# Spreading the fetched key pairs inside a chunk and cutting the value and output products into pieces

## Chip, core, metric

One NeuronCore of a Trainium2 chip runs the whole program. The metric is the device time of one execution in microseconds (us); several executions are timed and their median is given. The profile is one further execution, taken by the hardware profiler. TensorE (PE) multiplies matrices into PSUM banks; its weight loads are listed as PEld. VectorE (DVE), ScalarE (ACT) and GpSimd (POOL) work elementwise, and SyncE (SP) issues nearly all DMAs.

## The reference

Attention with squared ReLU instead of softmax feeds a gated unit with a causal convolution over five rows. B = 8, S = 3200, D = 256, and the query and key width is 64.

```python
scores = z @ z.T / S                      # queries and keys are the same z
attn = np.maximum(scores, 0) ** 2
x = u * (attn @ v)
gate = sigmoid(sum(conv_w[k] * x[t - 4 + k] for k in range(5)))
out = (gate * (x @ w_val)) @ w_out
```

All is float32. The kernel keeps that precision by splitting each operand of a product into a high part and a remainder and multiplying three combinations, called terms.

## The kernel before, in words

**Tiling.** The 3200 rows of a batch are 25 tiles of 128. Queries are taken in seven chunks of 4, 4, 4, 4, 3, 3, 3 tiles (the last batch: 4, 4, 4, 4, 4, 3, 2), so a product has 512, 384 or 256 columns. Keys are taken in 13 pairs of tiles (the last has one tile). A **step** is one chunk of queries with one pair of keys; 8 x 7 x 13 steps follow each other in one order written out by hand (`steps`, L762; the loop from L883), and `place` (L253) gives a pair's position in its chunk.

**Computed and fetched steps.** Scores are symmetric. A **computed** step multiplies queries and keys on TensorE (`scores`, L376), takes ReLU and square on ScalarE (L523, L524), splits into `ah` (ScalarE's cast, L526, or VectorE's, L528) and `al` (VectorE, L532), and, where a later chunk will need the mirrored block, turns it on VectorE (L431) and stores it in DRAM (L453). A **fetched** step (`mirrored`, L419) loads that block into `m` (L468) and only splits it, without scores. Steps `halves` and `split` do half of each. In the order before, pairs stand by number, so the fetched ones, which are the low ones, stand at the head of a chunk: 0, 2, 4, 6, 8, 9 and 11 of them in chunks 0 to 6 of the batches 1 to 6. Two exceptions are `new_first` (L248: chunk 3 of the last batch has them at the end) and the last chunk of all.

**One step on TensorE.** At step s TensorE multiplies the weights of step s with v into two accumulator banks `acc0`, `acc1` (12 products in slots of the chunk's width) and makes the scores of step s + 3 (`AHEAD`). Scores contract over 64 rows only, so two of them run side by side in the upper and the lower 64 rows of the array (`side_by_side`, L342, products at L350). So that the form need not change, the products with v are then done in 64-row form too, in two halves: `attend` part 0 lets the upper rows fill one bank and the lower rows the other, part 1 swaps them. Before part 1, `turn_round` (L361) makes TensorE wait until part 0 is done with the banks. If the pair at s + 3 is fetched, the step has no scores and runs with the full 128 rows (`attend_whole`, L566, the branch `if not halved`, L893).

**What else stands in the steps.** For the chunk before, `gated` (L591, `x`) multiplies the accumulators by u on VectorE at the end of its last step, which frees the banks for the next chunk; then come the convolution (L637), the value product (`value`, in two parts at step 5, or `value_whole`, L674) into the banks `misc`, and the gate (L642, L687 to L696). For the chunk before that, the output product stands at step 0 (`project`, two parts with one term of scores between them, or `project_whole`, L729), and ScalarE copies the result (`ob`, L748) at steps 1 and 2. `zq` is the chunk's queries in the order that a product reads contiguously (`z_order`, L225), written three steps before the chunk (five before chunk 0); where `has_copy` (L218) is false the scores read them strided from `zhl`. All other work hangs on steps through `at_step` (L777), in the order of the queues; `m` is fetched six steps before it is used, three before its split.

Of the kernel before, what the change touches and what calls it, by code (L numbers as in the profile page):

```python
# [17 lines left out]
def attn_glu_kernel(  # L18
# [30 lines left out]
    B, S, D = u.shape  # L49
# [195 lines left out]
    def own(b, c, x):  # L245
        return all_firsts[b][c] // 2 + x

    def new_first(b, c):  # L248


        return b == B - 1 and c == 3

    place = {}  # L253
    for b in range(B):
        for c in range(n_chunks):
            order = list(range(NP))
            if two_pairs(b, c):
                order.append(order.pop(own(b, c, 1)))
            if new_first(b, c):
                new = [i for i in order if sum(pairs[i]) > all_firsts[b][c]]  # L260
                new.sort(key=lambda i: pairs[i][0] < all_firsts[b][c])
                order = new + [i for i in order if i not in new]
# [141 lines left out]

    mirror, m_in, turned_, to_keep = {}, {}, {}, []

    def keeps(b, c, g):

        return c < g and (b > 0 or c > 1 or (c == 1 and g >= 5))
# [9 lines left out]
    def mirrored(b, c, i):  # L419
        return all(keeps(b, all_homes[b][t][0], c) for t in range(pairs[i][0], sum(pairs[i])))  # L420

    def turn(b, c, i, a):

# [130 lines left out]
                out_.append((acc, vp[:, j, hs], ap_[:, j], first and j == m == 0, last and j == n - 1 and m == 2))  # L554
        return out_

    def attend(b, c, i, part):

        p = place[b, c, i]
        x = (p + part) % 2  # L560
        sides = (attend_list(b, c, i, h, part == 0 and p == 0, part == 1 and p == NP - 1) for h in (x, 1 - x))
        turn_round("acc", sides, part)

    def attend_whole(b, c, i, h):
        for out_, st, mv, first, last in attend_list(b, c, i, h, place[b, c, i] == 0, place[b, c, i] == NP - 1):
# [88 lines left out]
                )  # L654
        return out_

    def value(b, c, part):
        if part == 0:
            pvs[b, c] = [ps.tile([P, 512], F32, name=f"misc{e}", bufs=1) for e in range(DH)]
        sides = (value_list(b, c, e, part == 0, part == 1) for e in (part, 1 - part))  # L660
        turn_round("misc", sides, part)

    def two_banks(spare, names="misc"):

# [49 lines left out]
    def project(b, c, part):  # L714
        if part == 0:
            pos[b, c] = [ps.tile([P, 512], F32, name=f"misc{x}", bufs=1) for x in range(DH)]
        sides = (project_list(b, c, x, part == 0, part == 1) for x in (part, 1 - part))
        turn_round("misc", sides, part)

    def project_whole(b, c, spare=False):  # L720
        pos[b, c] = two_banks(spare, "acc" if spare else "misc")
# [47 lines left out]
    def project_at(b, c):  # L769

        return 2 if (b, c) == (0, 2) else 0

    todo = {}
# [39 lines left out]
    for b in range(B):  # L813
        for c in range(n_chunks):
            s0 = start(b, c)
            nxt = s0 + NP
            for h in range(DH):
                for part in range(2):
                    at_step(max(s0 + U_LOAD[b > 0][c], 2) + 2 * h + part, u_load, b, c, h, part)
            if (b, c) != LAST:  # L820
                for r, fn, args in BEHIND:
                    late = b == c == 0 and fn in (gate_value, gate_value_high, gate_value_low)
                    at_step(nxt + (min(r + FIRST_VALUE - VALUE, FIRST_LAST[r]) if late else r), fn, b, c, *args)
                for x in range(DH):
                    at_step(nxt + project_at(*steps[nxt][:2]) + 1 + x, out_copy_before, b, c, x)
            at_step(max(s0 + U_PREP[b > 0][c], 6), u_prep, b, c)

            met = start(b, 0) + all_firsts[b][c] // 2 - AHEAD
            if has_copy(b, c):
                for x in range(2):  # L830
                    at_step(s0 - (5 if c == 0 or new_first(b, c) else 3), z_order, b, c, x)
            if b == 0:
                met -= c == 1
                at_step(met - 5, z_load, b, c)
                early = 1 if c == 0 else 0
                at_step(met - 3 - early, z_turn, b, c)
                at_step(met - 2 - early, z_high, b, c)
                at_step(met - 1 - early - (c >= 2), z_low, b, c)
            else:
                s1 = Z_FROM[b][c] + start(b - 1, 4)  # L840
                at_step(s1, z_load, b, c)
                late = 1 if b == 1 else 0
                at_step(s1 + late + 3, z_turn, b, c)
                at_step(s1 + late + 4, z_high, b, c)
                at_step(s1 + late + 5, z_low, b, c)
            for i in range(NP):
                if mirrored(b, c, i) or halves(b, c, i) or split(b, c, i):
                    at_step(s0 + place[b, c, i] - AHEAD - FETCH + (new_first(b, c) and halves(b, c, i)), m_fetch, b, c, i, first=True)
# [27 lines left out]
        for j in range(n + 1):  # L876
            at_step(first + j // step, next, fn, None)

    held = []
    with tc.manual_schedule():  # L880
        zeros = sb.tile([P, CW], F32R, name="zeros", tag="gvl", bufs=1)
        nc.vector.memset(f32(zeros), 0.0)
        for s in range(min(todo), END + 1):  # L883
            b, c, i = steps[s] if s >= 0 else (0, 0, 0)
            p = s % NP if s >= 0 else s
            ahead = steps[s + AHEAD] if 0 <= s + AHEAD < N else None
            halved = ahead and not mirrored(*ahead)
            terms = list(range(3))
# [3 lines left out]
            behind = steps[s - NP][:2] if s >= NP and p == (FIRST_VALUE if s < 2 * NP else VALUE) else None  # L892
            if not halved:  # L893
                if before:
                    project_whole(*before)
                for h in range(DH if 0 <= s < END else 0):
                    attend_whole(b, c, i, h)
                if behind:
                    for e in range(DH):
                        value_whole(*behind, e)  # L900
            else:
                if before:
                    project(*before, 0)
                    scores(*ahead, terms[:1])
                    project(*before, 1)
                    terms = terms[1:]
                if s >= NP and p == 0 and not before:

                    scores(*ahead, terms)
                    for h in range(DH):  # L910
                        attend_whole(b, c, i, h)
                    terms = ()
                elif s >= 0:
                    attend(b, c, i, 0)
                if behind:
                    value(*behind, 0)
                if terms:
                    scores(*ahead, terms)
                    if s >= 0:
                        attend(b, c, i, 1)  # L920
                if behind:
                    value(*behind, 1)
            if p == NP - 1:
                for h in range(DH):
                    gated(b, c, h)
                while held:
                    held.pop(0)()
# [85 lines left out]
```

## Time and profile before

| what | value |
|---|---|
| median of 3 timed runs | 2292.95 us (2292.73 to 2294.2) |
| the profiled execution, first to last instruction (span) | 2290.8 us |
| granted TensorE clock | 1.000 |
| DMA | 466.39 MB, mean 204 GB/s |

The profiled execution is known by its span alone. In the rows of the profile, an engine's busy time is given with its share of the span and its number of instructions; a group of instructions has its line, engine, operation, output and inputs, shape and count, then busy time and the mean duration of one in ns, and after the second bar the idle time just before them with what ended it. A row of waits reads: engine, tile and line that waited, what it waited for, us in total, times, longest. A row of the timeline reads: start and length in us, engine, line, operation, tiles, shape, count, and in brackets the idle time before. A row of a stretch gives its length and the busy time of PE, PEld, DVE, ACT and POOL with instruction counts, then the clock and the DMA's share and rate.

### The profile page before, as it was taken

Reading aid. Unit: us, or ns where it says so; the run is one execution under the profiler, and the core shown is the slowest. Engines: PE = TensorE matmul, PEld = TensorE weight load, DVE = VectorE, ACT = ScalarE, POOL = GpSimd, SP = SyncE. Lnnn points to the kernel's source line nnn. Section 1 sums busy time; section 2 is a strip of 40 time slices with the busy share of each in tenths; the row PEclk is TensorE's granted clock in tenths of the full one; section 3 lists DMA queues with packets and bytes.
Section 4 is the critical chain, followed back from the end, with each engine's and each line's share of the span. In section 5 each row is a group of like instructions: output and inputs, shape, how many; then the busy total and the mean of one; then the engine's idle time right before and its main releaser. Section 6 shows DMA issues by size and latency. Waiting matters only on the chain.

```text
span 2290.8 us, 47245 instructions
## 1 busy us (share of the span) xinstructions
PE 2283.8 (100%) x18625; PEld 2004.0 (87%) x18625; DVE 1818.1 (79%) x2393; ACT 1777.2 (78%) x2404; POOL 55.7 (2%) x108
## 2 busy tenths in 40 slices
PE   9999999999999999999999999999999999999999
PEld 7888988889888998889988899888998889988889
DVE  7877888788878878788787887888877887778776
ACT  8988778776888768887688776887768877687765
POOL 0000000000000000000000000000000000000000
PEclk9999999999999999999999999999999999999999
DMA  7265897778977889688887789868897788966753
GB/s 133 65 158 149 213 261 206 205 199 246 255 185 202 213 246 251 171 211 223 242 237 191 198 226 247 229 187 207 236 239 214 199 222 233 237 189 171 197 150 100
DMA packets 688592, 466.39 MB, mean 204 GB/s; under 512 B 355313, under 2 KB 639217, under 8 KB 688369
## 3 DMA queue, kind: packets, MB, share of 16 engines
q1 hardware_dynamic: 687168, 463.10, 76.4%
q8 instruction: 146, 2.39, 0.4%
q14 instruction: 78, 0.63, 0.1%
q10 hardware_dynamic: 1200, 0.26, 0.1%
HBM read 251.73 MB, written 211.48 MB: 202 GB/s over the span
## 4 chain that ended last, share of the span: by engine, by line
PE 96%; ACT 1%; DVE 1%; SPq 1%; DMA 1%; issue 0%; DVEq 0%; ACTq 0%
PE acc L350 45%; PE acc L566 29%; PE s L350 10%; PE misc L350 6%; PE misc L729 4%; PE misc L674 2%; SPq L166 0%; DMA u_raw<-in_u_dram 0%; ACT a L524 0%; SPq L292 0%; ACT a L523 0%; ACT ah L526 0%; DVE al L532 0%; DMA v_raw<-in_v_dram 0%; DMA z_raw<-in_z_dram 0%
## 5 line engine op out<-in xcount | busy, mean ns | idle before, releaser
L350 PE MATMUL acc<-ah,v_hl 64*128 64x512 f32 (+1 forms) x6624 | 1071.4, 375 | 0.7 <-DVE v_hl L308 0.7
L350 PEld LDWEIGHTS acc<-ah,v_hl 64*128 64x128 f32 x6624 | 620.1, 184 | 112.2 <-issue 11.7
L566 PE MATMUL acc<-ah,v_hl 128*128 128x384 f32 (+2 forms) x2288 | 639.6, 355 | 0.2 <-DVE x L596 0.2
L350 PE MATMUL acc<-al,v_hl 64*128 64x512 f32 (+1 forms) x3312 | 626.3, 374 | 0.0
L532 DVE TENSOR_TENSOR al<-a,ah 128x1024 fp32r<-128x1024 f32 (+3 forms) x387 | 422.9, 1093 | 223.1 <-ACT ah L526 215.3
L523 ACT ACTIVATE a<-s 128x1024 f32<-128x1024 f32 (+3 forms) x387 | 356.0, 920 | 146.1 <-PE s L350 144.5
L566 PEld LDWEIGHTS acc<-ah,v_hl 128*128 128x128 f32 x2288 | 417.5, 188 | 47.3 <-ACT a L486 5.7
L532 DVE TENSOR_TENSOR al<-m,ah 128x768 fp32r<-128x768 f32 (+2 forms) x303 | 307.9, 1024 | 121.3 <-ACT ah L526 120.6
L566 PE MATMUL acc<-al,v_hl 128*128 128x384 f32 (+2 forms) x1144 | 402.9, 352 | 0.0
L524 ACT ACTIVATE a<-a 128x1024 f32<-128x1024 f32 (+3 forms) x387 | 371.3, 959 | 12.3
L526 ACT CAST ah<-m 128x768 fp32r<-128x768 f32 (+2 forms) x303 | 266.7, 892 | 145.6 <-DMA m<-mir 108.7
L350 PEld LDWEIGHTS acc<-al,v_hl 64*128 64x128 f32 x3312 | 312.6, 184 | 46.9 <-DVE al L532 0.6
L526 ACT CAST ah<-a 128x1024 fp32r<-128x1024 f32 (+3 forms) x350 | 333.6, 953 | 11.1
L431 DVE STREAM_TRANSPOSE turned<-a 128x1024 f32<-128x1024 f32 (+3 forms) x318 | 320.1, 1011 | 25.6 <-DMA mir<-turned 24.7
L637 DVE SCALAR_TENSOR_TENSOR gate<-x,cw,gate 128x512 f32<-128x512 f32 (+2 forms) x448 | 303.5, 678 | 4.5 <-ACT gate L635 0.3
L350 PE MATMUL s<-zq,zhl 64*128 64x512 f32 (+3 forms) x2046 | 259.4, 356 | 0.0
L566 PEld LDWEIGHTS acc<-al,v_hl 128*128 128x128 f32 x1144 | 215.2, 188 | 15.1 <-DVE al L532 0.2
L350 PEld LDWEIGHTS s<-zq,zhl 64*128 64x128 f32 x2046 | 184.9, 184 | 29.4
L642 ACT ACTIVATE gate<-gate 128x512 f32<-128x512 f32 (+2 forms) x112 | 65.4, 584 | 47.5 <-DVE gate L637 47.3
L596 DVE TENSOR_TENSOR x<-acc,ut 128x512 f32<-128x512 f32 (+2 forms) x112 | 67.4, 629 | 38.4 <-PE acc L350 25.4
L316 ACT CAST v_made<-v_raw 128x512 fp32r<-128x512 f32 x97 | 55.9, 576 | 39.5 <-DMA v_kept<-v_made 38.4
L691 ACT CAST gvh<-gv 128x512 fp32r<-128x512 f32 (+2 forms) x112 | 64.0, 572 | 27.5 <-DVE gv L687 27.2
(120 smaller groups left out, 2020.1 us busy)
## 6 DMA issues: line engine op xcount, KB each, us to landing
m<-mir SPq DMA_DIRECT2D x191, 384.0 KB, 4.8
mir<-turned SPq DMA_DIRECT2D x340, 192.0 KB, 4.0
mir<-turned SPq DMA_DIRECT2D x188, 256.0 KB, 4.3
m<-mir SPq DMA_DIRECT2D x94, 512.0 KB, 6.1
v_hl<-v_kept SPq DMA_DIRECT2D x84, 512.0 KB, 6.6
v_kept<-v_made SPq DMA_DIRECT2D x71, 512.0 KB, 5.3
u_raw<-in_u_dram SPq DMA_DIRECT2D x264, 64.0 KB, 3.4
out_dram<-ob SPq DMA_DIRECT2D x33, 512.0 KB, 4.1
```

What stands on the lines that cost most here:

```text
L350: ins = nc.tensor.matmul(out_, st[r], mv[r], start=first, stop=last)
L431: nc.vector.transpose(into[:, t : t + m], a[:, j * w : (j + m) * w].rearrange("p (t m x) -> p t m x", t=m, x=BLK))
L523: nc.scalar.activation(a.rearrange("p (j x) -> p j x", j=2), s[:, :, :each], AF.Relu, scale=scale)
L524: nc.scalar.activation(a, a, AF.Square)
L526: nc.scalar.copy(hi, a)
L532: nc.vector.tensor_tensor(lo, a, f32(hi), op=ALU.subtract)
L566: nc.tensor.matmul(out_, st, mv, start=first, stop=last)
L596: nc.vector.tensor_tensor(x[:, h, HALO : HALO + w], accs[b, c][h][:, :w], ut[b, c][:, h, :w], op=ALU.mult)
L637: nc.vector.scalar_tensor_tensor(g, tap, cw[:, h, k : k + 1], g, op0=ALU.mult, op1=ALU.add)
L642: nc.scalar.activation(g, g, AF.Sigmoid)
L691: nc.scalar.copy(gvs[b, c][0][:, e, :w], gv_[b, c, e][:, :w])
L729: nc.tensor.matmul(out_, st, mv, start=first, stop=last)
```

## The change

In the chunks whose number of fetched pairs is a key of `MIRRORED_AT`, the fetched pairs take the listed places and the computed ones the rest, in their old order. `new_first` is gone. So most steps without scores (`lacks(s)`: the pair at s + 3 is fetched) now lie between the steps with scores.

A step without scores now runs in halves too when it is one of a chunk's `value_places` or `project_places`, or stands alone between two steps that do (`by_halves`). Between its two halves stands a piece of a product: the value product of the chunk before, cut into 2, 4 or 5 pieces over the steps 4 to 8 without scores, or part 1 of the output product, cut into as many pieces as there are such steps among 1 and 2, plus one at step 0 (part 0 and all terms of the scores then stand there without the one-term gap). A step without scores and without a piece does its first half and leaves its second (`left`) for the next step. Longer stretches without scores and pieces keep the 128-row form.

Around this, `zq` of these chunks is written five steps ahead, and the last two places of the chunk before read strided. The gate's steps move back by one or two where the last value piece is at step 7 or 8, the output copies go to step 2 where the output product ends there, and `attend` picks its side by a running switch.

```diff
     def has_copy(b, c, i=None):
-        if i is not None and new_first(b, c + 1) and place[b, c, i] == NP - 1:
+        if i is not None and place[b, c, i] >= NP - 2 and c < n_chunks - 1 and spread(b, c + 1):
             return False
...
+    MIRRORED_AT = {
+        2: (8, 9),
+        4: (7, 8, 9, 10),
+        6: (4, 7, 8, 9, 10, 11),
+        7: (4, 5, 7, 8, 9, 10, 11),
+        8: tuple(range(4, 12)),
+        9: tuple(range(4, 13)),
+    }
...
+    def spread(b, c):
+        n = sum(mirrored(b, c, i) for i in range(NP))
+        return n in MIRRORED_AT
...
+            if spread(b, c):
+                fetched = [i for i in order if mirrored(b, c, i)]
+                computed = [i for i in order if not mirrored(b, c, i)]
+                at_ = MIRRORED_AT[len(fetched)]
+                order = [(fetched if p in at_ else computed).pop(0) for p in range(NP)]
...
-    def attend(b, c, i, part):
+    way = [0]
+
+    def attend(b, c, i, part, again=False):
         p = place[b, c, i]
-        x = (p + part) % 2
+        if part and not again:
+            way[0] = 1 - way[0]
+        x = way[0]
...
-        turn_round("acc", sides, part)
+        turn_round("acc", sides, part and not again)
...
+    def cut(sides, piece, pieces):
+        out_ = []
+        for mms in sides:
+            lo, hi = (len(mms) * x // pieces for x in (piece, piece + 1))
+            out_.append(mms[lo:hi])
+        return out_
...
+    def lacks(s):
+        return s + AHEAD >= N or mirrored(*steps[s + AHEAD])
...
+    PIECES = {
+        2: ((0, 0, 1), (1, 0, 1)),
+        4: ((0, 0, 2), (0, 1, 2), (1, 0, 2), (1, 1, 2)),
+        5: ((0, 0, 2), (0, 1, 2), (1, 0, 3), (1, 1, 3), (1, 2, 3)),
+    }
+
+    def value_places(b, c):
+        s0 = start(b, c)
+        at_ = [p for p in range(4, 9) if lacks(s0 + p)] if (b, c) > (0, 1) and spread(b, c) else []
+        return at_ if len(at_) in PIECES else []
+
+    def project_places(b, c):
+        s0 = start(b, c)
+        return [p for p in (1, 2) if lacks(s0 + p)] if (b, c) > (0, 2) and spread(b, c) else []
+
+    def by_halves(s):
+        if s < 0 or not lacks(s):
+            return True
+        b, c, p = *chunk_of(s), s % NP
+        return p in value_places(b, c) or p in project_places(b, c)
...
+    GATE = {
+        7: {6: 7, 7: 8, 8: 9, 9: 9},
+        8: {6: 8, 7: 8, 8: 9, 9: 9},
+    }
...
-                    at_step(s0 - (5 if c == 0 or new_first(b, c) else 3), z_order, b, c, x)
+                    at_step(s0 - (5 if c == 0 or spread(b, c) else 3), z_order, b, c, x)
...
-            halved = ahead and not mirrored(*ahead)
+            halved = by_halves(s) or (by_halves(s - 1) and by_halves(s + 1))
...
+                if before and ends:
+                    project(*before, 0)
+                    scores(*ahead, terms)
+                    terms, fill = [], [(project, *before, 1, 0, len(ends) + 1)]
+                elif before:
                     project(*before, 0)
                     scores(*ahead, terms[:1])
                     project(*before, 1)
                     terms = terms[1:]
+                if p in ends:
+                    fill = [(project, *steps[s - 2 * NP][:2], 1, 1 + ends.index(p), len(ends) + 1)]
+                if piece:
+                    fill = [(value, *behind, *piece)]
+                    behind = None
...
+                for fn, *args in fill:
+                    fn(*args)
+                if s >= 0 and not whole:
+                    left.append((b, c, i))
+                if terms or fill or behind:
+                    for n in range(len(left)):
+                        attend(*left.pop(0), 1, again=n > 0)
```

`value` and `project` take the piece and pass their products through `cut`; only the first piece of part 1 turns the banks round.

More of the change, by code (lines that the diff above doesn't have):

```diff
@@ L246, in own, with keeps, mirrored @@
         return all_firsts[b][c] // 2 + x
-    def new_first(b, c):
-        return b == B - 1 and c == 3
+    MIRRORED_AT = {
[6 more added lines that the diff above has]
+    }
+    def keeps(b, c, g):
+        return c < g and (b > 0 or c > 1 or (c == 1 and g >= 5))
+    def mirrored(b, c, i):
+        return all(keeps(b, all_homes[b][t][0], c) for t in range(pairs[i][0], sum(pairs[i])))
+    def spread(b, c):
+        n = sum(mirrored(b, c, i) for i in range(NP))
+        return n in MIRRORED_AT
     place = {}
@@ L258, in attn_glu_kernel @@
                 order.append(order.pop(own(b, c, 1)))
[L259 to L262, printed above, removed]
+            if spread(b, c):
[3 more added lines that the diff above has]
+                order = [(fetched if p in at_ else computed).pop(0) for p in range(NP)]
             if b == B - 1 and c == n_chunks - 1:
@@ L655, in value_list, with value @@
         return out_
-    def value(b, c, part):
-        if part == 0:
+    def cut(sides, piece, pieces):
[4 more added lines that the diff above has]
+        return out_
+    def value(b, c, part, piece=0, pieces=1):
+        if part == piece == 0:
             pvs[b, c] = [ps.tile([P, 512], F32, name=f"misc{e}", bufs=1) for e in range(DH)]
-        sides = (value_list(b, c, e, part == 0, part == 1) for e in (part, 1 - part))
-        turn_round("misc", sides, part)
+        sides = [value_list(b, c, e, part == 0, part == 1) for e in (part, 1 - part)]
+        turn_round("misc", cut(sides, piece, pieces), part and piece == 0)
     def two_banks(spare, names="misc"):
@@ L712, in project_list, with project @@
         return out_
-    def project(b, c, part):
-        if part == 0:
+    def project(b, c, part, piece=0, pieces=1):
+        if part == piece == 0:
             pos[b, c] = [ps.tile([P, 512], F32, name=f"misc{x}", bufs=1) for x in range(DH)]
-        sides = (project_list(b, c, x, part == 0, part == 1) for x in (part, 1 - part))
-        turn_round("misc", sides, part)
+        sides = [project_list(b, c, x, part == 0, part == 1) for x in (part, 1 - part)]
+        turn_round("misc", cut(sides, piece, pieces), part and piece == 0)
     def project_whole(b, c, spare=False):
@@ L822, in attn_glu_kernel @@
                     late = b == c == 0 and fn in (gate_value, gate_value_high, gate_value_low)
-                    at_step(nxt + (min(r + FIRST_VALUE - VALUE, FIRST_LAST[r]) if late else r), fn, b, c, *args)
+                    if late:
+                        r = min(r + FIRST_VALUE - VALUE, FIRST_LAST[r])
+                    elif fn in (gate_value, gate_value_high, gate_value_low):
+                        r = GATE.get(max(value_places(*chunk_of(nxt)), default=VALUE), {}).get(r, r)
+                    at_step(nxt + r, fn, b, c, *args)
+                ends = project_places(*chunk_of(nxt))
                 for x in range(DH):
-                    at_step(nxt + project_at(*steps[nxt][:2]) + 1 + x, out_copy_before, b, c, x)
+                    at_step(nxt + (2 if len(ends) > 1 else project_at(*chunk_of(nxt)) + 1 + x), out_copy_before, b, c, x)
             at_step(max(s0 + U_PREP[b > 0][c], 6), u_prep, b, c)
@@ L847, in attn_glu_kernel @@
                 if mirrored(b, c, i) or halves(b, c, i) or split(b, c, i):
-                    at_step(s0 + place[b, c, i] - AHEAD - FETCH + (new_first(b, c) and halves(b, c, i)), m_fetch, b, c, i, first=True)
+                    at_step(s0 + place[b, c, i] - AHEAD - FETCH, m_fetch, b, c, i, first=True)
         if b == 0:
@@ L877, in attn_glu_kernel @@
             at_step(first + j // step, next, fn, None)
-    held = []
+    held, left = [], []
     with tc.manual_schedule():
@@ L886, in attn_glu_kernel @@
             ahead = steps[s + AHEAD] if 0 <= s + AHEAD < N else None
-            halved = ahead and not mirrored(*ahead)
-            terms = list(range(3))
+            places, ends = (value_places(b, c), project_places(b, c)) if s >= 0 else ((), ())
+            piece = PIECES[len(places)][places.index(p)] if p in places else None
+            halved = by_halves(s) or (by_halves(s - 1) and by_halves(s + 1))
+            terms = [] if lacks(s) else list(range(3))
             if s in (-AHEAD, 0):
@@ L891, in attn_glu_kernel @@
             before = steps[s - 2 * NP][:2] if s >= 2 * NP and p == project_at(b, c) else None
-            behind = steps[s - NP][:2] if s >= NP and p == (FIRST_VALUE if s < 2 * NP else VALUE) else None
+            behind = steps[s - NP][:2] if s >= NP else None
+            if p != (FIRST_VALUE if s < 2 * NP else VALUE) or places:
+                behind = behind if piece else None
             if not halved:
+                assert not left
                 if before:
@@ L901, in attn_glu_kernel @@
             else:
-                if before:
+                fill, whole = [], False
+                if before and ends:
[3 more added lines that the diff above has]
+                elif before:
                     project(*before, 0)
@@ L911, in attn_glu_kernel @@
                         attend_whole(b, c, i, h)
-                    terms = ()
+                    terms, whole = (), True
                 elif s >= 0:
@@ L923, in attn_glu_kernel @@
             if p == NP - 1:
+                assert not left
                 for h in range(DH):
```

8 lines of the change are left out of this document (2 added, 6 removed).

## The prediction

> **What bounds the kernel now.** I read the head of the page first, then the chain that ended last, then the waits of TensorE.
>
> ```profile
> span 2290.8 us, 47245 instructions
> PE 2283.8 (100%) x18625; PEld 2004.0 (87%) x18625; DVE 1818.1 (79%) x2393; ACT 1777.2 (78%) x2404; POOL 55.7 (2%) x108
> PE 96%; ACT 1%; DVE 1%; SPq 1%; DMA 1%; issue 0%; DVEq 0%; ACTq 0%
> PE misc L357 <- DVE zeros L882: 1.5, 1, 1.5
> ```
>
> TensorE is busy for the whole span, carries 96% of the chain, and its longest recorded wait, 1.5 us, lies at the start. So no other engine's work has to shrink; only what TensorE itself spends beyond its products can go. The ends of matmuls are modelled, which paints small gaps over, so I read starts in the timeline instead. A row "x2" of a 64-row form is two half-array matmuls side by side, one slot; a 128-row matmul is one slot too. Here the form changes, once into 128 rows and once out of it:
>
> ```profile
> 670.82 0.39 PE L350 MATMUL acc<-ah,v_hl 64*128 64x512 f32 x2
> 671.13 0.50 PE L566 MATMUL acc<-ah,v_hl 128*128 128x512 f32 x1
> 671.47 0.40 PE L566 MATMUL acc<-al,v_hl 128*128 128x512 f32 x1
> 671.70 0.63 PE L566 MATMUL acc<-ah,v_hl 128*128 128x512 f32 x2
> ...
> 683.48 0.39 PE L566 MATMUL acc<-ah,v_hl 128*128 128x512 f32 x1
> 683.80 0.50 PE L350 MATMUL acc<-ah,v_hl 64*128 64x512 f32 x2
> 684.14 0.40 PE L350 MATMUL acc<-al,v_hl 64*128 64x512 f32 x2
> 684.37 0.63 PE L350 MATMUL acc<-ah,v_hl 64*128 64x512 f32 x4
> ```
>
> A slot of 512 columns takes about 0.227 us from start to start in either form (671.47 to 671.70; 684.14 to 684.37). At a change of form the slot before it takes 0.31 or 0.32 us and the slot behind it 0.34: 0.65 instead of 0.45, so **a change costs 0.20 us**. The narrow slots say the same; these are the first and the last of the 96 changes that the starts show:
>
> ```profile
> 6.61 0.40 PE L357 MATMUL misc<-zeros 128*128 128x512 f32 x1
> 6.94 1.67 PE L350 MATMUL s<-zhl 64*128 64x512 f32 x12
> ...
> 2255.56 0.34 PE L350 MATMUL acc<-ah,v_hl 64*128 64x384 f32 x2
> 2255.83 0.45 PE L566 MATMUL acc<-ah,v_hl 128*128 128x384 f32 x1
> 2256.11 0.34 PE L566 MATMUL acc<-al,v_hl 128*128 128x384 f32 x1
> ```
>
> The last one: 0.27 + 0.28 us where two 384-column slots take 2 x 0.174, again 0.20. The 96 changes together cost 19 us.
>
> **What goes: 74 changes.** I count runs of 128 rows from the step order. A step is in 128-row form when the pair three steps ahead is fetched. Before, each of batches 1 to 6 has six such runs: steps 10 and 11 of chunk 0; then from step 10 of chunks 1, 2, 3, 4 and 5 into the head of the next chunk. That is 12 changes a batch. Batch 0 has 12, batch 7 has 9, and three stand at the very start: 72 + 12 + 9 + 3 = 96, as in the trace. After, batches 1 to 6 keep one run, from step 9 of chunk 5 to step 7 of chunk 6 (11 fetched pairs have no entry in MIRRORED_AT): 2 changes each. Batch 0 keeps the two heads of chunks 1 and 2 (4), batch 7 keeps its chunk 5, which fetches 10 pairs (3): 12 + 4 + 3 + 3 = 22. Gain: 74 x 0.20 = **14.8 us**. The products themselves are the same slots in the other form, and the groups by shape show no difference in their mean duration (the overlapping durations, not the slots):
>
> ```profile
> L350 PE MATMUL acc<-ah,v_hl 64*128 64x384 f32 x1672 | 239.8, 336 | 0.0
> L566 PE MATMUL acc<-ah,v_hl 128*128 128x384 f32 x1364 | 355.5, 336 | 0.0
> ```
>
> [...]
>
> **What is added: turns.** A step in halves multiplies each row half into one accumulator bank, then waits until the other half is done with it and changes over (turn_round). By the step order the turns of acc rise from 420 to 615, those of misc from 56 to 93. What one costs depends on what lies between the halves:
>
> ```profile
> 669.30 0.52 PE L350 MATMUL s<-zq,zhl 64*128 64x256 f32 x6
> 669.65 0.40 PE L350 MATMUL acc<-ah,v_hl 64*128 64x512 f32 x2
> 669.89 0.40 PE L350 MATMUL acc<-al,v_hl 64*128 64x512 f32 x2
> ...
> 2249.44 0.47 PE L350 MATMUL s<-zq,zhl 64*128 64x192 f32 x6
> 2249.75 0.36 PE L350 MATMUL acc<-ah,v_hl 64*128 64x384 f32 x2
> 2249.95 0.33 PE L350 MATMUL acc<-al,v_hl 64*128 64x384 f32 x2
> ...
> 633.72 0.39 PE L350 MATMUL s<-zq,zhl 64*128 64x512 f32 x2
> 633.95 0.38 PE L350 MATMUL misc<-w_out_hi,gvl 64*128 64x256 f32 x2
> 634.17 0.28 PE L350 MATMUL misc<-w_out_lo,gvh 64*128 64x256 f32 x2
> ```
>
> With 0.35 us of other work between them the first slot takes 0.24 instead of 0.227: 0.01 us. With 0.31 us it takes 0.20 instead of 0.174: 0.03. With one slot alone (0.23 us, the output product of an earlier chunk around one term of scores) it takes 0.22 instead of 0.12: 0.10. The new pieces give 0.45 us (a third of a value half, 2 slots of 0.227), 0.68 (a half of it), 0.48 (a third of an output half, 4 x 0.12); the shortest is 2 x 0.174 = 0.35. So an added acc turn costs from 0 to 0.03; I take 0.01, the nearest row: 195 x 0.01 = 2.0 us. The new misc turns have a whole half of attention products between them, 1.0 us or more, and cost nothing, but output products around one term rise from 17 to 23: 6 x 0.10 = 0.6 us. Where a step without scores has no filling (step 3 of chunks 4 and 5), its second half is put off behind the next step's filling and shares that turn, so no unfilled turn arises.
>
> Because zq is now written five steps ahead, the last two places of a chunk read their queries in strided form: 54 more steps, 162 slots. These are the two forms:
>
> ```profile
> L350 PE MATMUL s<-zq,zhl 64*128 64x512 f32 x1368 | 195.7, 387 | 0.0
> L350 PE MATMUL s<-zhl,zhl 64*128 64x512 f32 x228 | 33.3, 393 | 0.5 <-ACT a L516 0.5
> ```
>
> 6 ns each: 162 x 0.006 = 1.0 us at most, which I take.
>
> **What moves, and what hides it.** The two output halves of the head of chunks 3, 4 and 5 no longer stand together, so less work lies between the last attention product of a chunk and the first of the next, which needs both accumulator banks read by VectorE (x):
>
> ```profile
> 632.42 0.39 PE L350 MATMUL acc<-ah,v_hl 64*128 64x512 f32 x2
> 632.85 1.29 DVE L596 TENSOR_TENSOR x<-acc,ut 128x512 f32<-128x512 f32 x2 [2.93 <-PE acc L350]
> 635.12 0.40 PE L350 MATMUL acc<-ah,v_hl 64*128 64x512 f32 x2
> 802.36 0.33 PE L566 MATMUL acc<-ah,v_hl 128*128 128x384 f32 x1
> 803.33 1.02 DVE L596 TENSOR_TENSOR x<-acc,ut 128x384 f32<-128x384 f32 x2
> ```
>
> Both reads are over 1.72 us after the last product; the next came 2.70 after it. At the 22 changed heads it is due after 0.23 + 12 x 0.12 + 3 x 0.227 = 2.35 us, in chunk 5 (384 columns) after 0.17 + 1.44 + 0.52 = 2.13. Cover left: 0.6 us. With VectorE one instruction behind, as at 803.33, the reads end 1.99 us after, still inside 2.13. I count it at nothing.
>
> The reorder takes fetched steps from the chunks' heads, where ScalarE is fullest, and the pieces move the gating products and the output copies by up to two steps. SP's queue gets m's fetches at other steps, always three steps ahead of their cast as before, and behind no more mirror stores than now. The chunk that has no fetched pair at its head already is chunk 0:
>
> ```profile
> 581.00:626.50 45.50, 45.50 (x432) 38.67 (x428) 40.96 (x54) 39.87 (x49) 0.10 (x1) 1.00 0.95 259
> L526 ACT CAST ah<-a 128x1024 fp32r<-128x1024 f32 (+3 forms) x350 | 333.6, 953 | 11.1
> ```
>
> ScalarE needs 39.9 of 45.5 us there. Three of that chunk's casts are VectorE's; given back (3 x 0.95) ScalarE would need 42.7, still less than TensorE takes. So chunk 1 led by eight computed steps should run, on less slack. A gating product that waits for the last piece holds VectorE for a step, within the three steps of lead.
>
> **Sum.** -14.8 + 2.0 + 0.6 + 1.0 = -11.2 us on the profiled span: 2290.8 to 2279.6. The median of the runs stands 2.15 us above that span; carried along, **2281.7 us**. The bounds of turns (0 to 5.9) and strided reads (0 to 1.0) give 2278.7 to 2285.6; the halves' other forms could differ by a little either way, so I start at 2278.
>
> **Rivals.** (1) *Weights late at the heads of chunks 1 and 2.* This is the least lead of a step in batch 3, from VectorE's last remainder to TensorE's product that reads it:
>
> ```profile
> 955.92 0.68 DVE L503 TENSOR_TENSOR al<-a,ah 128x512 fp32r<-128x512 f32 x1
> 957.98 0.39 PE L566 MATMUL acc<-al,v_hl 128*128 128x512 f32 x1
> ```
>
> It ends at 956.60 and is read at 957.98, 1.4 us later. If the long computed run uses that up and TensorE waits 0.5 us at each of 14 heads, 7 us go: 2288.7. For it: ScalarE's 42.7 of 45.5. Against: the output product adds 2.9 us of cover at each head. 0.13. (2) *Banks late.* One VectorE instruction of 1.2 us more ahead of x makes each of 22 heads 0.6 us late, 13 us: 2294.9. Against: 0.6 us of cover. 0.05. (3) *The turns are not hidden*, the case that ends slower. If a filling does not cover a turn, each of the 195 costs the 0.10 us of row 634.17: 19.5 instead of 2.0, 2299.2. It decides at 13.2 / 195 = 0.07 us a turn: above that the change loses. For it: the one-slot turn. Against: 0.35 us is enough in two rows. 0.05. [...] (4) *Less goes than 0.20 us a change.* If only the 0.11 us behind the change is its own (0.34 at 671.47 against 0.227) and the 0.09 ahead of it is a wait that stays, 74 x 0.11 = 8.1 us go and 3.6 come: 2288.4. Against: slots of 64 rows with no change near, such as 669.89, show no such gap. 0.05. [...] (5) *It does not do what it says*: the reorder works, but the steps without scores still run in 128 rows. Five or six runs a batch remain, and about 2293 us. 0.02.
>
> **Chances.** Forecast 0.70; rivals 0.13, 0.05, 0.05, 0.05, 0.02. A measurement here tells about 0.2%, 4.6 us, from no change, so faster means under 2288.4. The forecast, most of (1) and half of (4) lie there: 0.83. Within 0.2%: the rest of these, most of (2), and (5): 0.11. Slower: (3) and a little of (2): 0.06. The range, 2278 to 2289, takes in the forecast's bounds, (4) and (1).
>
> **What will show it.** Starts in TensorE's timeline: 22 changes of form instead of 96, each still 0.20 us; first slots behind a filled turn at 0.23 to 0.25 us. TensorE's waits by release should stay near nothing; a row of acc waiting for x would be (2), one for ah or al (1), and slots of 0.33 behind value or output pieces (3).

## The result and the profile after

| what | before | after |
|---|---|---|
| median of 5 timed runs, us | 2292.73 (2291.56 to 2294.2) | 2308.58 (2307.25 to 2310.54) |
| profiled span, us | 2290.8 | 2305.0 |

The kernel became slower: the ratio is 1.0069 (95% interval 1.0057 to 1.0082). The head of the page and the chain that ended last, of after:

```profile
span 2305.0 us, 53339 instructions
PE 2279.9 (99%) x21673; PEld 2021.7 (88%) x21673; DVE 1818.9 (79%) x2391; ACT 1771.5 (77%) x2406; POOL 66.8 (3%) x108
PE 63%; ACT 11%; DVE 9%; DMA 8%; issue 5%; SPq 3%; DVEq 0%; ACTq 0%
```

VectorE and ScalarE do as much work as before and TensorE is still painted 99% busy. But the chain, 96% TensorE before, now runs a third of its length over the other engines and over DMAs. The waits of TensorE name two places (row: who waited for what, us in total, times, longest):

```profile
PE acc L367 <- DVE al L542: 12.4, 14, 1.6
PE misc L367 <- DVE gvl L718: 5.1, 9, 0.9
```

**Where they stand.** The ends of matmuls are modelled, so I took all starts of TensorE's timeline, laid the slots of the step order under them (0.227, 0.174 and 0.120 us for 512, 384 and 256 columns, the medians from start to start in before and in after; 0.20 for each change of form) and subtracted, step by step. What is over is the **excess**. Before it is 11.2 us in all, after 39.9: 28.7 more. The largest parts, summed over the eight batches:

| us | before | after | in batches 1 to 6 after |
|---|---|---|---|
| chunk 4, step 4 | 0.7 | 11.5 | 1.6 to 2.0 each |
| chunk 2, step 0 | 1.1 | 5.6 | 0.6 to 1.1 each |
| chunk 5, step 4 | 0 | 3.7 | 0.6 each |
| chunk 0, step 0 | 1.4 | 3.7 | 1.4 in batch 1, 1.1 in batch 4 |

These four are 21.3 of the 28.7 us. Six smaller ones of 0.7 to 1.2 us (step 0 of chunks 1 and 5, steps 8 and 11 of chunk 3, 10 and 11 of chunk 6) add 5.2, and 2.2, net, are left for turns, strided reads and everything else.

**The changes of form did go.** One of the 22 that are left, in TensorE's timeline of after:

```profile
832.82 0.35 PE L367 MATMUL acc<-ah,v_hl 64*128 64x384 f32 x2
833.11 0.44 PE L580 MATMUL acc<-ah,v_hl 128*128 128x384 f32 x1
833.38 0.34 PE L580 MATMUL acc<-al,v_hl 128*128 128x384 f32 x1
833.56 0.52 PE L580 MATMUL acc<-ah,v_hl 128*128 128x384 f32 x2
```

0.29 + 0.27 us instead of 2 x 0.174: 0.21. So 74 x 0.20 = 14.8 us went, and 28.7 came: 13.9 slower, against 14.2 in the spans. (The excess is what is left of the starts, so this sum tests only the bookkeeping.)

**Chunk 4, step 4, in batch 2.** TensorE first, then VectorE:

```profile
783.82 0.62 PE L367 MATMUL acc<-ah,v_hl 64*128 64x384 f32 x4
786.03 0.44 PE L367 MATMUL acc<-al,v_hl 64*128 64x384 f32 x2 [1.58 <-DVE al L542]
...
787.47 0.40 PE L367 MATMUL misc<-xh,w_val_hi 64*128 64x512 f32 x2
787.71 0.33 PE L367 MATMUL acc<-ah,v_hl 64*128 64x384 f32 x2
787.88 0.34 PE L367 MATMUL acc<-al,v_hl 64*128 64x384 f32 x2
```

```profile
781.30 0.96 DVE L542 TENSOR_TENSOR al<-a,ah 128x768 fp32r<-128x768 f32 x1 [1.60 <-ACT ah L536]
782.17 0.97 DVE L441 STREAM_TRANSPOSE turned<-a 128x768 f32<-128x768 f32 x1
783.07 1.18 DVE L637 TENSOR_TENSOR xl<-x,xh 128x1024 fp32r<-128x1024 f32 x1
784.17 0.97 DVE L599 STREAM_TRANSPOSE ut<-u_raw 128x768 f32<-128x768 f32 x1
785.06 0.92 DVE L542 TENSOR_TENSOR al<-m,ah 128x768 fp32r<-128x768 f32 x1
```

The first row is two slots: the last of step 3's first half and the first of step 4's. The next slot was due at 783.82 + 2 x 0.174 = 784.17 and starts at 786.03, when VectorE has just finished the step's remainder (785.06 + 0.92 = 785.98). Ahead of it on VectorE's queue stand the value product's input (`xl`) and the next `ut`; ahead of those, VectorE itself had idled for ScalarE. The last three rows of TensorE answer another step: behind the value piece the accumulator turns, and the slots there take 0.24 and 0.17 us, so this turn is hidden.

ScalarE's timeline of the same stretch shows why it is late:

```profile
750.54 0.63 ACT L656 ACTIVATE gate<-gate 128x512 f32<-128x512 f32 x1 [3.71 <-DVE gate L651]
...
754.07 0.62 ACT L333 CAST v_made<-v_raw 128x512 fp32r<-128x512 f32 x1 [2.29 <-DMA v_kept<-v_made]
...
762.34 0.62 ACT L713 CAST gvh<-gv 128x512 fp32r<-128x512 f32 x1 [2.33 <-DVE gv L709]
...
768.12 0.62 ACT L713 CAST gvh<-gv 128x512 fp32r<-128x512 f32 x1 [0.44 <-DVE gv L709]
...
781.79 0.82 ACT L536 CAST ah<-m 128x768 fp32r<-128x768 f32 x1
782.52 1.18 ACT L770 COPY ob<-misc 128x256 f32<-128x256 f32 x4
783.57 0.86 ACT L536 CAST ah<-m 128x768 fp32r<-128x768 f32 x1
```

In the stretch in which chunk 3 splits its fetched pairs ScalarE idles in line (the rows show it held by the gate, by a store of v and by `gv`), then works from 768.12 to 784.43 without a gap: the computed steps at the head of chunk 4 and what stands between them. It comes out behind: step 4's cast, the one at 781.79, ends at 782.61, and VectorE gets to its remainder at 785.06. The waits of ScalarE, of before and then of after, say the same for the whole run:

```profile
ACT a L523 <- PE s L350: 144.5, 126, 4.7
ACT gate L642 <- DVE gate L637: 47.3, 39, 2.6
ACT gvh L691 <- DVE gv L687: 27.2, 36, 1.4
```

```profile
ACT gate L656 <- DVE gate L651: 110.3, 55, 4.1
ACT gvh L713 <- DVE gv L709: 106.9, 68, 4.6
ACT a L533 <- PE s L367: 43.4, 54, 3.9
```

An idle ScalarE that waits for TensorE's scores is one that has caught up. These 144 us fell to 43; the idle time now stands ahead of `gate` and `gvh`, and the casts behind them in the queue come after it. What ends an idle time need not be what makes it, as one tap will show.

**Chunk 2, step 0, in batch 3**, TensorE and then VectorE:

```profile
968.29 0.28 PE L367 MATMUL misc<-w_out_hi,gvh 64*128 64x256 f32 x2
968.99 0.39 PE L367 MATMUL misc<-w_out_hi,gvl 64*128 64x256 f32 x2 [0.42 <-DVE gvl L718]
```

```profile
966.45 1.23 DVE L542 TENSOR_TENSOR al<-a,ah 128x1024 fp32r<-128x1024 f32 x1 [1.47 <-ACT ah L536]
967.59 0.76 DVE L451 STREAM_TRANSPOSE turned<-a 128x256 f32<-128x256 f32 x2
968.28 0.65 DVE L718 TENSOR_TENSOR gvl<-gv,gvh 128x512 fp32r<-128x512 f32 x1
```

Here it is the output product that waits, for the remainder of its own input: 0.70 us from start to start where 0.12 are usual (the four slots ahead of it start at 967.81, 967.93, 968.05 and 968.17).

### The profile page after: what moved, and what is told of

It reads as the page before. It is cut to its first block, busy times and chain, and to the rows that moved or that the text cites. A ratio compares the mean times of both kernels' runs of the same rounds, so it can differ in the third digit from the quotient of the medians.

```text
span 2305.0 us, 53339 instructions
## 1 busy us (share of the span) xinstructions
PE 2279.9 (99%) x21673; PEld 2021.7 (88%) x21673; DVE 1818.9 (79%) x2391; ACT 1771.5 (77%) x2406; POOL 66.8 (3%) x108
## 4 chain that ended last, share of the span: by engine, by line
PE 63%; ACT 11%; DVE 9%; DMA 8%; issue 5%; SPq 3%; DVEq 0%; ACTq 0%
PE acc L367 40%; PE acc L580 8%; PE s L367 7%; PE misc L367 6%; ACT a L534 3%; ACT a L533 3%; ACT ah L536 2%; DMA m<-mir 2%; DVE al L542 2%; DMA mir<-turned 2%; DVE turned L441 2%; DMA z_raw<-in_z_dram 2%; DMA v_kept<-v_made 1%; SPq L463 1%; SPq L166 1%
## 5 line engine op out<-in xcount | busy, mean ns | idle before, releaser
L367 PE MATMUL acc<-ah,v_hl 64*128 64x512 f32 (+1 forms) x9656 | 1532.5, 370 | 0.9 <-DVE v_hl L325 0.6
L367 PEld LDWEIGHTS acc<-ah,v_hl 64*128 64x128 f32 x9656 | 914.4, 184 | 127.6 <-issue 1.9
L367 PE MATMUL acc<-al,v_hl 64*128 64x512 f32 (+1 forms) x4828 | 913.2, 370 | 12.7 <-DVE al L542 12.4
L367 PEld LDWEIGHTS acc<-al,v_hl 64*128 64x128 f32 x4828 | 463.7, 184 | 79.3 <-DVE al L542 19.9
L536 ACT CAST ah<-m 128x768 fp32r<-128x768 f32 (+2 forms) x303 | 269.3, 893 | 167.2 <-DMA m<-mir 127.7
L536 ACT CAST ah<-a 128x1024 fp32r<-128x1024 f32 (+3 forms) x352 | 334.9, 951 | 11.2
L580 PE MATMUL acc<-ah,v_hl 128*128 128x384 f32 (+2 forms) x772 | 195.9, 332 | 0.2 <-DVE x L610 0.2
L656 ACT ACTIVATE gate<-gate 128x512 f32<-128x512 f32 (+2 forms) x112 | 65.5, 584 | 110.4 <-DVE gate L651 110.3
L713 ACT CAST gvh<-gv 128x512 fp32r<-128x512 f32 (+2 forms) x112 | 64.1, 573 | 106.9 <-DVE gv L709 106.9
L580 PEld LDWEIGHTS acc<-ah,v_hl 128*128 128x128 f32 x772 | 137.6, 188 | 4.7 <-issue 1.5
L580 PE MATMUL acc<-al,v_hl 128*128 128x384 f32 (+2 forms) x386 | 127.7, 331 | 0.1
L367 PE MATMUL misc<-w_out_hi,gvl 64*128 64x256 f32 x676 | 101.5, 288 | 5.1 <-DVE gvl L718 5.1
L367 PE MATMUL misc<-w_out_lo,gvh 64*128 64x256 f32 x676 | 98.0, 279 | 0.0
L367 PE MATMUL misc<-w_out_hi,gvh 64*128 64x256 f32 x676 | 97.7, 279 | 0.0
```

The lines of the kernel that those rows point to most:

```text
L367: ins = nc.tensor.matmul(out_, st[r], mv[r], start=first, stop=last)
L536: nc.scalar.copy(hi, a)
L580: nc.tensor.matmul(out_, st, mv, start=first, stop=last)
L656: nc.scalar.activation(g, g, AF.Sigmoid)
L713: nc.scalar.copy(gvs[b, c][0][:, e, :w], gv_[b, c, e][:, :w])
```

## The experiments

Excess is meant as above, without the changes of form, which are taken at 0.20 us each in every kernel. "C4s4" is step 4 of chunk 4, summed over the batches, and so on. Medians stand beside a median of before on the same chip of 2291.7 to 2293.2 us. Of the times that the expectations name, those of one by one and no left half (theory A of each) came within 2 us, and that of one tap (above 2300) came. In the other nine runs the median lies between the two times, or outside both (wide only, gate sooner), and the columns say more than the median.

| kernel | median us | ratio, 95% | changes of form | excess | C4s4 | C5s4 | C2s0 | C0s0 |
|---|---|---|---|---|---|---|---|---|
| before | 2292.73 | | 96 | 11.2 | 0.7 | 0 | 1.1 | 1.4 |
| after | 2308.58 | 1.0057 to 1.0082 | 22 | 39.9 | 11.5 | 3.7 | 5.6 | 3.7 |
| reorder alone | 2304.20 | 1.0035 to 1.0065 | 88 | 23.9 | gone | gone | 3.0 | 4.7 |
| value at once | 2299.61 | 1.0017 to 1.0038 | 86 | 20.5 | 0.8 | gone | 3.0 | 2.9 |
| wide only | 2292.99 | 0.9992 to 1.0010 | 52 | 19.9 | gone | gone | 4.8 | 1.4 |
| `ut` later | 2303.17 | 1.0032 to 1.0066 | 22 | 34.7 | 6.0 | 0.6 | 4.8 | 6.0 |
| value whole in 3 | 2303.53 | 1.0027 to 1.0061 | 38 | 33.4 | 4.7 | 3.8 | 5.7 | 4.4 |
| gate sooner | 2321.04 | 1.0108 to 1.0138 | 22 | 55.3 | 12.1 | 3.7 | 1.1 | 4.8 |
| old order in 1, 2 | 2310.35 | 1.0060 to 1.0090 | 54 | 37.1 | 11.9 | 3.8 | 1.1 | 7.0 |
| narrow only | 2300.18 | 1.0019 to 1.0039 | 68 | 21.1 | gone | 3.7 | 1.1 | 4.1 |
| one by one | 2284.44 | 0.9949 to 0.9978 | 52 | 13.1 | gone | gone | 1.1 | 2.3 |
| no sigmoid | 2300.74 | 1.0024 to 1.0051 | 22 | 33.4 | 10.3 | 0.6 | 5.3 | 3.5 |
| one tap | 2300.85 | 1.0017 to 1.0047 | 22 | 32.2 | 9.9 | 3.8 | 1.1 | 4.9 |
| no left half | 2302.93 | 1.0029 to 1.0063 | 48 | 29.9 | 1.7 | 0.5 | 6.5 | 3.4 |

**Reorder alone.** The order of after, without any piece:

```diff
-        return at_ if len(at_) in PIECES else []
+        return []
...
-        return [p for p in (1, 2) if lacks(s0 + p)] if (b, c) > (0, 2) and spread(b, c) else []
+        return []
```

> The new order of the pairs, but no pieces: steps without scores run in 128 rows again and value and output products stand at their old steps. 88 changes of form instead of 22, so 66 x 0.20 = 13 us more of them, and about 2 us of turns less. Theory A (the order itself makes TensorE wait: ScalarE cannot use the fetched stretch in mid-chunk because it may lead by three steps only, and is late at the next chunk's head): the waits stay, about 2308.6 + 11 = 2320 us. Theory B (the pieces make it wait: value and gate come late and hold ScalarE and VectorE in line): the 24 us of waits go, about 2296 us.

Ratio 1.0050. The order by itself costs 12.7 us of excess (23.9 against 11.2), mostly in small portions at chunk heads (0, 2, 4 and 5). The wait at step 4 of chunks 4 and 5 is not in it.

**Value at once.** The output pieces stay, the value product is not cut (the first of the two edits above).

> The new order, the output product still in pieces at steps 0 to 2, but the value product whole at step 5 and the gate at its old steps; 86 changes of form, 13 us more of them than after. Theory A: the waits stay, about 2320 us. Theory B by the late value product: the waits go, about 2297 us. If only the thinner cover by the cut output product counts, this stays near 2320 us while the order alone is near 2296 us.

4.6 us less than reorder alone with almost as many changes of form: the output pieces do no harm. Step 4 is free of its wait here too. But without value pieces steps 3 to 8 run in 128 rows, so this kernel also takes away the half that step 3 leaves over; it can't say which of the two matters.

**Wide only and narrow only.** The new order and the pieces in chunks 1 to 3 (512 columns), or only in chunks 4 and 5 and those of seven fetched pairs:

```diff
-        7: (4, 5, 7, 8, 9, 10, 11),
-        8: tuple(range(4, 12)),
-        9: tuple(range(4, 13)),
```

> The change for chunks with 2, 4 and 6 fetched pairs only; chunks 4 and 5 (and chunks 5 and 6 of batch 0) keep the old order and the 128-row runs. 52 changes of form, 6 us more than after. Theory A with its place at the heads of chunks 4 and 5: their waits at step 4 (10.8 + 3.7 us more than before) go, about 2299 us, and the wait at the head of chunk 2 (4.5 us) stays. If the lead is lost inside chunk 3 and only shows in chunk 4, the wait turns up elsewhere and the time is about 2312 us.

Wide only ends where before does: 44 changes of form fewer, 8.8 us, and 8.7 us more excess, most of it at step 0 of chunk 2 and steps 8, 11 and 12 of chunk 3.

```diff
-        2: (8, 9),
-        4: (7, 8, 9, 10),
-        6: (4, 7, 8, 9, 10, 11),
```

> The change for chunks with 7, 8 and 9 fetched pairs only (chunks 4 and 5, and two of batch 0); chunks 1 to 3 keep the old order. 68 changes of form, 9 us more than after. If chunk 4's waits come from chunk 3's late gate, they go, and those at the heads of chunks 0 and 2 too: about 2297 us. If they are chunk 4's own (computed steps of 384 columns at a head that still has the 512-column gate to do), they stay: about 2308 us.

TensorE's products of chunk 4 now stand in exactly the order of after (batches 1 to 7), but behind a chunk 3 in the old order, and its wait at step 4 is gone. Step 4 of chunk 5 keeps its 3.7 us. So the wait of chunk 4 needs what the new chunk 3 does before it.

**`ut` later.** `U_PREP` puts the turn of u behind step 4's remainder: step 2 in chunk 4, step 5 in chunk 5.

```diff
-    U_PREP = ((1,) * n_chunks, (10, 10, 3) + (1,) * (n_chunks - 3))
+    U_PREP = ((1,) * n_chunks, (10, 10, 3, 1, 2, 5, 1))
```

> The changed kernel with one VectorE instruction moved: the transpose of u (ut, about 0.97 us) of chunks 4 and 5 stands one and four steps later, behind the remainder that TensorE waits for at step 4. If VectorE's own queue is what is late there, each of the 7 + 6 waits shrinks by up to 0.97 and 0.6 us, up to 10 us: about 2299 us. If ScalarE's casts are late anyway, nothing changes: 2308 us.

The 0.97 us of `ut` ahead of `al` on VectorE's queue are worth 0.9 us a batch in chunk 4 (11.5 to 6.0) and all of it in chunk 5 (3.7 to 0.6). Some comes back at step 0 of chunk 0 (3.7 to 6.0).

**Value whole in 3.** The value product in chunk 3's steps is not cut (`c != 3` in `value_places`).

> The changed kernel, but in chunk 3 of every batch the value product stands whole at step 5 and its gate at the old steps; 38 changes of form, 3 us more than after. If the gate that chunk 3 does late (steps 8 and 9) is what makes ScalarE and VectorE late at the head of chunk 4, the waits at step 4 of chunk 4 (11.5 us in all) fall to about 1 us: 2301 us. If chunk 4's own pieces cause them (output product cut, value product from step 4 on), they stay: 2312 us.

C4s4 falls to 4.7 though chunk 4 is untouched. The edit moves the value pieces, the gate and `gvh` of chunk 3 together; with it the idle time that `gv` ends on ScalarE, from step 4 of chunk 3 to step 1 of chunk 4 in batches 1 to 6, falls from 18.1 to 1.6 us. So the late value product of chunk 3 is part of the late line, and 4.7 us are not its doing.

**Gate sooner.** The gate of chunk 1's steps is moved ahead, against the wait at the head of chunk 2:

```diff
     GATE = {
+        6: {10: 9, 11: 10},
```

> The changed kernel, but where the last value piece stands at step 6 (chunk 1) the second half of the gate's cast and remainder (gvh, gvl) each come one step sooner. If the head of chunk 2 waits because gvl stands behind the remainders of computed steps in VectorE's queue, its 5.6 us shrink to about 1 us: 2304 us. If VectorE is late there whatever the order, they stay: 2308 us.

The wait at the head of chunk 2 goes (5.6 to 1.1), and 12 us appear at steps 11 and 12 of chunk 1: `gvh` now stands on ScalarE ahead of its input. The wait moved within a queue and grew.

**Old order in chunks 1 and 2** (keys 2 and 4 taken out of `MIRRORED_AT`).

> The change for chunks with 6, 7, 8 and 9 fetched pairs only; chunks 1 and 2 keep the old order. 54 changes of form, 6.4 us more than after. If the long run of computed steps from chunk 0 into chunk 1 is the cause of the waits at the heads of chunks 0, 1 and 2 (7.5 us more than before), these go: about 2307.5 us, with the wait at step 4 of chunk 4 as in after. If they come from elsewhere they stay: 2315 us.

The head of chunk 2 is free (1.1), at the price of 32 changes of form, and step 0 of chunk 0 has 7.0. C4s4 stays at 11.9: it does not come from the first chunks.

**No sigmoid and one tap.** Less work on ScalarE (the line of the sigmoid taken out) and less on VectorE (the taps behind the first taken out):

```diff
-        nc.scalar.activation(g, g, AF.Sigmoid)
```

> The changed kernel without the sigmoid (left out; the gate goes on unsquashed): 65 us of ScalarE's work and its 110 us of waiting in line for VectorE's convolution go; VectorE's work stays. If ScalarE is what comes late, by its work and its waits in line, TensorE's 24 us of waits shrink to a few: about 2290 us. If VectorE's own load is the bound at the heads, they stay: above 2303 us.

```diff
-            nc.vector.scalar_tensor_tensor(g, tap, cw[:, h, k : k + 1], g, op0=ALU.mult, op1=ALU.add)
+            pass
```

> The changed kernel with the first of the five convolution taps alone (the other four left out): 305 us of VectorE's work go, eight instructions a chunk, and ScalarE no longer waits for them; ScalarE's own work stays. If VectorE's load at the heads is the root, TensorE's waits all but vanish: about 2285 us. If ScalarE's own work is, they stay: above 2300 us.

C4s4 stays in both (10.3 and 9.9): the work of either engine alone does not make it. Nor does the wait for the gate. These are ScalarE's waits in one tap, over the whole run:

```profile
ACT ah L536 <- DMA m<-mir: 166.7, 104, 4.4
ACT gvh L713 <- DVE gv L709: 96.3, 69, 4.3
ACT v_made L333 <- DMA v_kept<-v_made: 62.2, 22, 5.4
```

In after they are 127.7, 106.9 and 27.0 us, and 110.3 more for the gate; here the gate's are gone and DMAs hold ScalarE longer. In the stretch from step 4 of chunk 3 to step 1 of chunk 4, summed over batches 1 to 6 from ScalarE's timeline, it is idle for 66.2 us in after (the convolution ends 22.5 of them, `gv` 18.1, a store of v 13.0, a fetch of `m` 10.0), for 64.5 in one tap and for 72.3 in no sigmoid, where the convolution ends none of it. Narrow only, with chunk 3 in the old order, has 10.2. So the new chunk 3 leaves ScalarE idle there whichever wait comes last, and no run moves the fetches and stores to tell their part.

The wait at the head of chunk 2 goes with the taps (1.1) and stays without the sigmoid (5.3): there VectorE's load counts, at the end of chunk 1's long computed run. C5s4 goes with the sigmoid (0.6).

**One by one.** The fetched pairs of chunks 1 to 3 stand singly between computed ones, chunks 4 and 5 keep the old order, and nothing is cut:

```diff
     MIRRORED_AT = {
-        2: (8, 9),
-        4: (7, 8, 9, 10),
-        6: (4, 7, 8, 9, 10, 11),
-        7: (4, 5, 7, 8, 9, 10, 11),
-        8: tuple(range(4, 12)),
-        9: tuple(range(4, 13)),
+        2: (1, 4),
+        4: (1, 4, 6, 8),
+        6: (1, 3, 5, 7, 9, 11),
     }
```

(with both edits of reorder alone)

> Chunks 1, 2 and 3 take their fetched pairs one at a time between computed ones (places 1, 4 / 1, 4, 6, 8 / 1, 3, 5, 7, 9, 11), so each step without scores stands alone and runs in halves by leaving its second half to the next step. No pieces; value and gate at their old steps; chunks 4 and 5 keep the old order. 52 changes of form instead of 96: 8.8 us less than before, 2 us more turns. Theory A (late because computed steps stand together at the heads while fetched ones stand together where ScalarE cannot use them): no new waits, about 2286 us. Theory B (any step that leaves its half, or any departure from fetched pairs at the head, makes ScalarE and VectorE late): waits as in wide_only, 2293 us or more.

This is faster than both kernels: 0.9964 of before. 44 changes of form go (8.8 us) and 1.9 us of excess come: 6.9 less, and the span is 2283.9, 6.9 less. The chain that ended last, and ScalarE's waits:

```profile
PE 94%; ACT 2%; DVE 2%; DMA 1%; issue 1%; SPq 0%; DVEq 0%; ACTq 0%
```

```profile
ACT a L530 <- PE s L364: 165.7, 149, 4.7
ACT gate L653 <- DVE gate L648: 66.2, 49, 2.9
ACT gvh L710 <- DVE gv L706: 38.2, 37, 2.1
```

TensorE carries the chain again, and ScalarE's idle time stands where it has caught up (165.7 us ahead of `a`). The lone steps without scores put off their second halves here too, so a half put off does not by itself make TensorE wait. Against wide only, which has as many changes of form, both the order and the pieces differ; which of the two counts more, this run does not tell.

**No left half.** Step 3 of chunks 4 and 5 has neither scores nor a piece; in after it does its first half only. Here it runs whole:

```diff
-            halved = by_halves(s) or (by_halves(s - 1) and by_halves(s + 1))
+            halved = by_halves(s) or (by_halves(s - 1) and by_halves(s + 1) and not (c in (4, 5) and p == 3))
```

> Step 3 of chunks 4 and 5 runs whole in 128 rows instead of leaving its second half behind step 4's value piece, so that step 4 asks for its remainder six slots (6 x 0.174 = 1.04 us) later. It adds about 26 changes of form, 26 x 0.20 = 5.2 us. Theory A, the left half makes step 4's weights due earlier than VectorE's line can have them: the wait at chunk 4 step 4 falls from 11.5 us (1.6 to 2.0 a batch) by about 1.0 a batch to 4 to 6, that at chunk 5 step 4 (3.7, 0.61 a batch) goes; 2308.6 + 5.2 - 6.5 - 3.7 = 2303.6 us. Rival B, the line on ScalarE and VectorE is late by itself and slips with TensorE, whatever it does in step 3 (a second later is a second later for all): both waits stay at 11 and 3.7 us, 2313.8 us. Half and half (the first wait falls to 8, the second goes) would give 2306.6.

The same place in batch 2, TensorE and then VectorE, and after them one row of TensorE's waits and two of ScalarE's:

```profile
785.60 0.44 PE L367 MATMUL acc<-ah,v_hl 64*128 64x384 f32 x2
786.20 0.44 PE L367 MATMUL acc<-al,v_hl 64*128 64x384 f32 x2 [0.16 <-DVE al L542]
```

```profile
784.34 0.97 DVE L599 STREAM_TRANSPOSE ut<-u_raw 128x768 f32<-128x768 f32 x1
785.23 0.92 DVE L542 TENSOR_TENSOR al<-m,ah 128x768 fp32r<-128x768 f32 x1
```

```profile
PE acc L367 <- DVE al L542: 1.9, 6, 0.6
```

```profile
ACT gate L656 <- DVE gate L651: 124.8, 56, 5.0
...
ACT gvh L713 <- DVE gv L709: 105.8, 73, 4.6
```

The remainder is ready at 786.15, 0.17 us later than in after, and is read at once in both. But step 4 starts at 785.60 instead of 783.99: the six slots of step 3's second half (1.04 us) and the two changes of form around that step lie ahead of it now. Of these 1.61 us, 1.04 are the half, 0.40 the changes of form (2 x 0.20), and 0.17 the delay that the remainder has too. C4s4 falls from 11.5 to 1.7, further than the 4 to 6 expected, because the changes of form cover a part as well, and C5s4 falls from 3.7 to 0.5. The whole gains less: 3.0 of these 13.0 us come back elsewhere, at the head of chunk 2 and in chunk 6 of batch 0, and 26 more changes of form cost 5.2; the span is 4.1 us shorter than after's. The waits of ScalarE are at least as long as in after (`gvh` 105.8 against 106.9, `gate` 124.8 against 110.3): the line is as late as it was, and only the time at which TensorE asks has moved.

## Why the prediction was wrong

**The step that failed** is "What moves, and what hides it", which costed the moved steps and gates at nothing, "within the three steps of lead", and with it the half put off, which "What is added: turns" counted as a turn alone. The sum has no term for either. The runs show 28.7 us of added waiting, 14.5 of it at step 4 of chunks 4 and 5, and there two things act together.

1. *The half put off.* I saw that step 3 of chunks 4 and 5 has no filling and that its second half is put off, and treated this as a question of turns alone. But what is put off lets the next step's products come 6 x 0.174 = 1.04 us sooner, and these need weights that VectorE has not made. No left half shows it: 13.0 of the 28.7 us are at those two places and go with it (9.8 in chunk 4, 3.2 in chunk 5); of the 1.44 us by which step 4 then asks later, the 0.17 of the remainder's own delay left out, 0.40 are changes of form.
2. *Lead counted over a chunk.* 39.9 and 42.7 of 45.5 us are sums over a chunk, which say nothing of what stands in line: in batch 2 `al` starts at 785.06, behind `xl` (783.07) and `ut` (784.17), though its input was cast by 782.61. Over chunk 3's fetched pairs ScalarE stands still for some 11 us a batch (66.2 / 6), which it can't save up, as it may be no more than three steps ahead, and then it meets a row of computed steps without a gap (768.12 to 784.43). Narrow only (C4s4 gone) and value whole in 3 (4.7) show that the new chunk 3 makes the line late. How much of that is the order and how much the late value product, the gate, or the fetches and stores, is only partly separated (value whole in 3, one tap). `ut` later shows that one instruction of 0.97 us in the queue ahead is worth nearly its full length at TensorE (0.9 us a batch in chunk 4). Neither cause is enough: with the left half but the old chunk 3, and with the new chunk 3 but no left half, the wait is nearly gone.

**What held.** 74 changes went at 0.20 us each; of those that are left, the one at 832.82 takes 0.21. Turns and strided reads, forecast at 3.6 us, lie within the 2.2 us that no place of waiting claims. The cover of the banks held: TensorE's one recorded wait for `x` is 0.2 us, so rival (2) did not come. Rival (3), nearly all of the 0.06 given to a slower kernel, did not come either: turns stayed hidden (787.47 to 787.88), and the slowing has another cause. Rival (4) is out: at the 80 steps where a change of before stands no longer (six of after's 22 stand at new steps), the excess of after is 1.7 us in all, 0.02 each and not 0.09.

**Rival (1)** had the right kind, weights late, and part of the place: the head of chunk 2 took 4.5 us more, that of chunk 1 0.7. But there the output product waits for its own `gvl`, so it could not serve as cover, as I had argued against the rival; and what counted was VectorE's load (one tap) and the place of `gvl` in its queue (gate sooner), not ScalarE's 42.7 of 45.5 us, by which I judged it. I put it at 7 us and looked for it at heads of chunks alone; step 4 of chunks 4 and 5 was not examined.

**Open.** What makes ScalarE idle over chunk 3's fetched pairs is not settled (value whole in 3 still has 61.9 of the 66.2 us). Step 0 of chunk 0 costs from 1.4 to 7.0 us in these kernels, in other batches each time; no run isolates it. The waits at steps 10 and 11 of chunk 6 in batch 0 (over 4 us together, in no left half) were not tried. Nor was one by one joined with pieces in chunks 4 and 5, which on these numbers would need the chunk 3 of the former.

## What to carry to other kernels

Where work was put off, the products behind it asked for their inputs that much sooner (1.04 us at step 4 of chunk 4): check the lead of the next step, not only the cost of the one moved. Judge slack where the queue stands still, not by busy time over a stage; ScalarE had lead where it idled for TensorE (165.7 us ahead of `a` in one by one) and came out behind where it idled in the middle of its own line (66.2 us over chunk 3's fetched pairs in after, 10.2 in narrow only). The wait that ends an idle time need not be its cause: with the convolution's taps gone, other waits ended the same idle time (66.2 and 64.5 us). Spreading the stalls of form one at a time kept that lead, and got 8.8 us by it and paid 1.9, where the fuller change got 14.8 and paid 28.7.

## What the runs showed of the hardware

A change of form cost about the same whether there were 96 of them or 22: by the starts, 94 of before's and 20 of after's took 0.20 to 0.23 us, the other two, at 57 and 104 us of the span in both, 0.37 to 0.43. It took the place of a wait in no left half, where the changes around step 3 gave VectorE, at 2 x 0.20, 0.40 of the 1.61 us by which step 4 came later. Taking work off one engine hardly shortened the wait at step 4 of chunk 4 (one tap and no sigmoid, C4s4 9.9 and 10.3 of 11.5), while moving one instruction of 0.97 us behind the remainder in the queue took half of it away (`ut` later, 6.0).
